# A fixed order for the prologue, the first batch's values summed on GpSimd, queries loaded over ScalarE's queue, and a ring of three token blocks

## The chip, the cores and the metric

One core of a Trainium2 chip runs the whole program. The metric is the device time of one execution in microseconds, as a median of three runs. All arithmetic starts from float32 inputs; the large products are made from pairs of float32r values (a high part and a remainder), three products for each.

## The reference

```
k_p = k.reshape(B, H, Sp, 8, D).mean(axis=3)     # B, H, S, D = 8, 8, 576, 64; Sp = 72
v_p = v.reshape(B, H, Sp, 8, D).mean(axis=3)
attn = softmax(q @ k_p.T / sqrt(D))              # sum + 1e-9 in the denominator
x = (attn @ v_p) as tokens [B * S, H * D]        # 4608 x 512
x = (h - tanh(h)) @ w_out,   h = x @ w_in        # first layer, 512 -> 2048 -> 512
x = (h * cos(h)) @ w_out2,   h = x @ w_in2       # second layer, 512 -> 2048 -> 512
```

## The kernel before

The 4608 tokens are worked through in nine blocks of 512 (`NB`), and in each block over 16 steps `f` of 128 hidden columns (`NF`). A step of either layer makes 12 products into a hidden tile `h` (`emit_h`, line 553; `emit_h2`, line 747), an activation on ScalarE and VectorE (`g1_act`, `g1_rest`, `g_second`; `g2_a`, `g2_b`), and 12 products into four accumulators (`emit_out1`, line 591; `emit_out2`, line 775), two steps later (`LAG`). A finished block of the first layer is copied out of the accumulators (`evac1`, line 598) and stored to `x1s`, and the second layer loads it again (`x1_load`, `x1_split`, spread over the steps by `x1_next`).

Attention makes the first layer's tokens. A tile of up to 128 queries goes through `s1` (transposes of the queries, line 332, and a copy `qT`, line 334), `s2` in two halves (scores, line 346; row maximum, line 349; subtraction, line 353; exponential, line 355), `norm` (sum, add, reciprocal, multiply, lines 360 to 364), `s3` in two parts (transposes of the weights, lines 375 and 385, copies `ah`, `ar`), and, when its group of tiles is complete, `pv` four times (value products, line 406; copy `xh`, line 409; remainder `xl`, line 413). Batches 0 and 1 (`PV32`) make the value products in plain float32. Keys and values come as 8 x 64 rows and are summed by `pool_kv`: for batch 0 by one reduction on VectorE (line 266), for the others by three additions on GpSimd (lines 269, 270). `kprep` transposes the summed keys into `bd`; `place_v` puts the summed values into `vbd` and `vbr`, scaled by the columns of `mk`. Tokens go into `xh` and `xl`, a ring of `RING` columns; `xcols` cuts a stretch of tokens where the ring wraps, and `emit_h` makes a product for each piece.

The weights of the first layer arrive as 64-bit words and are converted on the way (`converter`, run step by step by `w1_tick`): ScalarE line 157, VectorE lines 166 and 168, ScalarE line 172, GpSimd line 149 or 162. Even steps' weights stay on chip (`RES`), odd ones (`STR`) go to DRAM and are streamed through a ring of two tiles each, `ri` and `ro`. The second layer's weights are converted during the first layer's blocks and loaded in the last one by `w2_resident`.

The prologue handles batch 0: its four tiles of 128 queries and the scores of the fifth (64 queries), and the key sums of batch 1. The rest of attention is a list of items; during each block `slot` hands out the items that are due, so that the next block's tokens are ready in time. Up to block 7 a planner with a cost model orders each engine's instructions out of this program (`MANUAL = 8`; from block 8 on the program's own order holds, by `tc.manual_schedule()`), and it may bring work of block 0 forward into the prologue. All loads are issued on SyncE's queue.

## Time and profile before

| what | us |
| --- | --- |
| median of 3 runs | 1791.51 |
| lowest and highest | 1791.44, 1793.8 |
| the profiled execution | 1789.61 |
| its span, first to last instruction | 1787.8 |
| TensorE busy in it | 1741.1 |
| VectorE, ScalarE, GpSimd busy | 1242.3, 1147.4, 276.0 |

The span is what the trace covers; the rest of the profiled execution's time lies around it. Busy time of an engine is the union of its instructions. PE stands for TensorE's matmuls, PEld for its weight loads, DVE for VectorE, ACT for ScalarE, POOL for GpSimd, SP for SyncE; L12 is line 12 of the kernel. Rows of a timeline give the start, the length and, in brackets, the idle time of the engine just before and what ended it.

### The profile page before, as it was taken

How to read it: one execution, taken by the hardware profiler on the slowest of the kernel's cores; microseconds unless marked ns; L12 is line 12 of the kernel's file. 1: busy time of each engine (PE TensorE's matmuls, PEld its weight loads, DVE VectorE, ACT ScalarE, POOL GpSimd, SP SyncE). 2: the span in 40 equal slices, each digit the busy share in tenths (PEclk: the TensorE clock that was granted, in tenths of full speed). 3: DMA queues.
4: the chain of work that ended last, by engine and by line, in shares of the span. 5: the costliest groups of instructions: out<-in, count | busy, mean ns of one | idle time of the engine just before them, and what ended most of it. 6: DMA issues, size and time to landing. Idle time of an engine off the chain costs nothing.

```text
span 1787.8 us, 23298 instructions
## 1 busy us (share of the span) xinstructions
PE 1741.1 (97%) x8344; PEld 1446.7 (81%) x8344; DVE 1242.3 (69%) x2109; ACT 1147.4 (64%) x2079; POOL 276.0 (15%) x342
## 2 busy tenths in 40 slices
PE   4989999999999999999999999999999999999999
PEld 3666878998888888889988888888888888888887
DVE  8689788778888887776666566566656665666555
ACT  4567666767677776765555666666666566666665
POOL 3754244213424131100000000000000000000000
PEclk9799999999999999999999999999999999999999
DMA  7565655545655564523278201010101010101000
GB/s 233 167 211 184 218 165 191 198 158 183 209 180 182 185 199 140 176 99 111 79 258 306 100 12 36 13 42 7 42 7 42 7 41 7 42 7 41 1 24 24
DMA packets 116403, 202.32 MB, mean 113 GB/s; under 512 B 45376, under 2 KB 61760, under 8 KB 116288
## 3 DMA queue, kind: packets, MB, share of 16 engines
q1 hardware_dynamic: 116288, 200.84, 33.9%
q8 instruction: 66, 1.08, 0.3%
q14 instruction: 49, 0.40, 0.1%
HBM read 156.76 MB, written 44.04 MB: 112 GB/s over the span
## 4 chain that ended last, share of the span: by engine, by line
PE 86%; DVE 5%; DMA 3%; ACT 3%; POOL 2%; issue 1%; SPq 0%; POOLq 0%; DVEq 0%; ACTq 0%
PE h L747 22%; PE acc L775 21%; PE h L553 19%; PE acc L591 18%; PE att L406 2%; PE att L346 2%; DMA kv<-in_k_dram 1%; POOL kv L269 1%; DVE cva L168 1%; PE att L375 1%; DMA raw<-in_moe_w_in_dram 1%; DVE w L576 1%; DMA raw<-in_moe_w_out_dram 1%; PE att L332 1%; DVE cva L166 0%
## 5 line engine op out<-in xcount | busy, mean ns | idle before, releaser
L747 PE MATMUL h<-xh,wi 128*128 128x512 f32 x1152 | 378.2, 389 | 0.0
L775 PE MATMUL acc<-wo,gh 128*128 128x512 f32 x1152 | 354.9, 389 | 0.1
L775 PEld LDWEIGHTS acc<-wo,gh 128*128 128x128 f32 x1152 | 216.2, 188 | 45.4 <-ACT gh L583 0.5
L747 PEld LDWEIGHTS h<-xh,wi 128*128 128x128 f32 x1152 | 216.4, 188 | 45.0
L758 DVE SCALAR_TENSOR_TENSOR r<-kk,h 128x512 f32<-128x512 f32 (+1 forms) x145 | 99.2, 684 | 181.9 <-ACT kk L756 181.4
L747 PE MATMUL h<-xl,wi 128*128 128x512 f32 x576 | 224.2, 389 | 0.0
L775 PE MATMUL acc<-wo,gl 128*128 128x512 f32 x576 | 224.2, 389 | 0.0
L766 ACT ACTIVATE r<-r 128x512 f32<-128x512 f32 (+1 forms) x145 | 91.4, 630 | 195.1 <-DVE r L760 195.1
L553 PE MATMUL h<-xh,wi 128*128 128x512 f32 (+1 forms) x704 | 205.9, 364 | 1.8 <-ACT wi L172 1.2
L553 PE MATMUL h<-xh,ri 128*128 128x512 f32 (+1 forms) x704 | 203.3, 360 | 0.0
L572 DVE SCALAR_TENSOR_TENSOR w<-u,h 128x512 f32<-128x512 f32 x144 | 98.3, 682 | 149.3 <-ACT th L565 149.0
L768 DVE TENSOR_TENSOR co<-co,h 128x512 f32<-128x512 f32 (+1 forms) x145 | 99.3, 685 | 117.9 <-ACT co L767 117.9
L591 PE MATMUL acc<-gh,wo 128*128 128x512 f32 x576 | 179.3, 393 | 0.0
L591 PE MATMUL acc<-gh,ro 128*128 128x512 f32 x576 | 177.9, 390 | 0.0
L755 ACT ACTIVATE kk<-h,bias_r 128x512 f32<-128x512 f32 (+1 forms) x145 | 99.5, 686 | 92.0 <-PE h L747 92.0
L564 ACT ACTIVATE u<-h 128x512 f32<-128x512 f32 x144 | 85.7, 595 | 103.9 <-PE h L553 103.5
L553 PEld LDWEIGHTS h<-xh,wi 128*128 128x128 f32 x704 | 126.4, 191 | 19.7 <-ACT wi L172 1.4
L553 PEld LDWEIGHTS h<-xh,ri 128*128 128x128 f32 x704 | 125.4, 190 | 17.2 <-POOL ri L162 0.4
L583 ACT ACTIVATE gh<-w 128x512 fp32r<-128x512 f32 x144 | 90.9, 631 | 74.7 <-DVE w L577 72.6
L584 DVE TENSOR_TENSOR gl<-w,gh 128x512 fp32r<-128x512 f32 x144 | 107.6, 747 | 28.7 <-ACT gh L583 25.9
L775 PEld LDWEIGHTS acc<-wo,gl 128*128 128x128 f32 x576 | 108.0, 188 | 22.5 <-DVE gl L584 0.2
L747 PEld LDWEIGHTS h<-xl,wi 128*128 128x128 f32 x576 | 108.0, 188 | 22.4
(157 smaller groups left out, 3376.0 us busy)
## 6 DMA issues: line engine op xcount, KB each, us to landing
ri<-s1i SPq DMA_DIRECT2D x64, 512.0 KB, 3.5
ro<-s1o SPq DMA_DIRECT2D x64, 512.0 KB, 3.7
raw<-in_moe_w_in_dram SPq DMA_DIRECT2D x32, 512.0 KB, 4.0
raw<-in_moe_w_out_dram SPq DMA_DIRECT2D x32, 512.0 KB, 4.1
x1s<-xe SPq DMA_DIRECT2D x36, 256.0 KB, 4.8
xr<-x1s SPq DMA_DIRECT2D x36, 256.0 KB, 3.0
out_dram<-xe SPq DMA_DIRECT2D x36, 256.0 KB, 2.0
kv<-in_k_dram SPq DMA_DIRECT2D x32, 256.0 KB, 4.0
```

The costliest lines, as they stand in the source:

```text
L553: nc.tensor.matmul(out=h[:, off:off + m], lhsT=wi[:, c, wsel, :], rhs=xt[:, r:r + m], start=(n == 0), stop=(n == 3 * KC - 1))
L564: nc.scalar.activation(out=u, in_=h, func=AF.Square)
L572: nc.vector.scalar_tensor_tensor(w, u, C2, h, op0=ALU.mult, op1=ALU.mult)
L583: nc.scalar.activation(out=gh[:, a:e], in_=w[:, a:e], func=AF.Copy)
L584: nc.vector.tensor_tensor(gl[:, a:e], w[:, a:e], gh[:, a:e].bitcast(F32), op=ALU.subtract)
L591: nc.tensor.matmul(out=acc[d], lhsT=wo[:, wsel, d * 128:(d + 1) * 128], rhs=gt, start=(f == 0 and n == 0), stop=(f == NF - 1 and n == 2))
L747: nc.tensor.matmul(out=h, lhsT=wi[:, c, wsel, :], rhs=xt[:, o:o + BLK], start=(n == 0), stop=(n == 3 * KC - 1))
L755: nc.scalar.activation(out=kk[:, a:e], in_=h[:, a:e], func=AF.Identity, bias=bias_r, scale=INV_2PI)
L758: nc.vector.scalar_tensor_tensor(r[:, a:e], kk[:, a:e], -PI2_HI, h[:, a:e], op0=ALU.mult, op1=ALU.add)
L766: nc.scalar.activation(out=r[:, a:e], in_=r[:, a:e], func=AF.Abs)
L768: nc.vector.tensor_tensor(co[:, a:e], co[:, a:e], h[:, a:e], op=ALU.mult)
L775: nc.tensor.matmul(out=acc[t], lhsT=gt[:, t * 128:(t + 1) * 128], rhs=wo[:, wsel, :], start=(f == 0 and n == 0), stop=(f == NF - 1 and n = ...
```

## The change

The ring holds 1536 columns instead of 1280, so a block always starts at a multiple of 512. To make room the mask of the first layer's activation overwrites its input `u`, the reloads of the first layer's result use the buffers `xe` of the result copies (and come three steps later), and the second layer's weights of the last two odd steps live in the ring tiles. The prologue runs in the program's own order, rewritten by hand; it ends with the four tiles of batch 0 that make the first 512 tokens. The fifth tile's scores and batch 1's key sums become items of block 0. Batch 0's values are summed on GpSimd. The queries of the four tiles are loaded by ScalarE's queue. An exponential on one column stands first on ScalarE, and tiles 2 and 3 have their own buffers for the exponentials, out of the space of `al`, which batches 0 and 1 don't use. Nine conversion steps are asked for in the prologue, where there were 26, of which the rule `w1_allowed` lets through the first six pieces. In the diff the removed lines of the old prologue are left out (they stand in the kernel above).

```diff
--- before.py
+++ after.py
@@ -49,7 +49,7 @@
     NP = H // 2
     BLK = 512
     NB = NT // BLK
-    RING = 1280
+    RING = 1536
     LAG = 2
     RES = [f for f in range(NF) if f % 2 == 0]
     STR = [f for f in range(NF) if f not in RES]
@@ -262,14 +262,15 @@
         else:
             n = GR if b in PV32 else 3 * GR
             o = vr[:n, c - NP, :]
-        if b == 0:
+        if b == 0 and which == "k":
             nc.vector.tensor_reduce(o, t[:n].rearrange("p (r d) -> p d r", r=POOL), axis=AX.X, op=ALU.add)
         else:
             for w in (POOL * D // 2, POOL * D // 4):
                 nc.gpsimd.tensor_tensor(t[:n, :w], t[:n, :w], t[:n, w:2 * w], op=ALU.add)
             nc.gpsimd.tensor_tensor(o, t[:n, :D], t[:n, D:2 * D], op=ALU.add)
-        if which == "k" and c == NKC - 1:
-            nc.scalar.activation(out=kp[:, :, D:2 * D], in_=kp[:, :, 0:D], func=AF.Copy)
+        if which == "k" and (c == NKC - 1 or (b == 0 and c == KSPLIT[0][1] - 1)):
+            c0 = (KSPLIT[1][0] if c == NKC - 1 else 0) if b == 0 else 0
+            nc.scalar.activation(out=kp[:, c0:c + 1, D:2 * D], in_=kp[:, c0:c + 1, 0:D], func=AF.Copy)
 
     def place_v(b):
         if b not in PV32 and b - 1 in PV32:
@@ -317,10 +318,10 @@
                     o = e * SP + x0 - h * SP
                     nc.scalar.activation(out=bd[p:p + D, h // 2, o:o + x1 - x0], in_=at[p:p + D, x0 - lo:x1 - lo], func=AF.Copy)
 
-    def load_q(t, pool=None, tag="qt", bufs=2):
+    def load_q(t, pool=None, tag="qt", bufs=2, queue=None):
         n = t["n"]
         qt = (pool or ap).tile([128, H * D], F32, tag=tag, name="qt", bufs=bufs)
-        nc.sync.dma_start(
+        (queue or nc.sync).dma_start(
             out=qt[:n].rearrange("p (h d) -> p h d", h=H),
             in_=q[t["b"], :, t["s"]:t["s"] + n, :].rearrange("h s d -> s h d"))
         t["qt"] = qt
@@ -334,10 +335,12 @@
         nc.scalar.activation(out=qT[:, :, :n], in_=at.rearrange("p (g n) -> p g n", g=NP)[:, :, :n], func=AF.Copy)
         t["qT"] = qT
 
+    first_e = {}
+
     def s2(t, half):
         n = t["n"]
         if half == 0:
-            t["e"] = eb[t["i"] % 2]
+            t["e"] = first_e.pop(t["i"], eb[t["i"] % 2])
             t["sm"] = ap.tile([128, H], F32, tag="sm", name="sm", bufs=2)
         e, sm, qT = t["e"], t["sm"], t["qT"]
         at = att_tile()
@@ -367,7 +370,8 @@
         n, e, g, o = t["n"], t["e"], t["g"], t["o"]
         if o == 0 and part == 0:
             g["ah"] = ap.tile([128, NP, 320], F32R, tag="ah", name="ah")
-            g["al"] = ap.tile([128, NP, 320], F32R, tag="al", name="al")
+            if t["b"] not in PV32:
+                g["al"] = ap.tile([128, NP, 320], F32R, tag="al", name="al")
             g["ar"] = ap.tile([3 * GR, NG, 320], F32R, tag="ar", name="ar")
         at = att_tile()
         if part == 0:
@@ -375,10 +379,10 @@
                 nc.tensor.transpose(at[:, p * 128:p * 128 + n], e[:n, main_rows(p)], ident[:n, :n])
             av = at.rearrange("p (c n) -> p c n", c=NP)[:, :, :n]
             ah = g["ah"][:, :, o:o + n]
-            al = g["al"][:, :, o:o + n]
             if t["b"] in PV32:
                 nc.scalar.activation(out=ah.bitcast(F32), in_=av, func=AF.Copy)
                 return None
+            al = g["al"][:, :, o:o + n]
             nc.scalar.activation(out=ah, in_=av, func=AF.Copy)
             return lambda: nc.vector.tensor_tensor(al, av, ah.bitcast(F32), op=ALU.subtract)
         for a in range(NG):
@@ -451,7 +455,15 @@
 
 
     t = tiles[n0]
-    item(lambda: kprep(0))
+    item(lambda t=t: s1(t), lambda t=t: load_q(t))
+    post_kv("k", 1, 0)
+    post_kv("k", 1, 1)
+    item(lambda t=t: s2(t, 0), apart=True)
+    post_kv("k", 1, 2)
+    post_kv("k", 1, 3)
+    item(lambda t=t: s2(t, 1))
+    post_kv("k", 1, 4)
+    item(lambda: kprep(0), apart=True)
     post(lambda t=t: norm(t))
     post_kv("v", 1, 0)
     item(lambda t=t: s3(t, 0))
@@ -567,14 +579,13 @@
 
     def g1_rest(h, u, th):
         s = cp.tile([128, BLK], F32, tag="t2", name="s")
-        m = cp.tile([128, BLK], F32, tag="t3", name="m")
         w = cp.tile([128, BLK], F32, tag="t4", name="w", bufs=2)
         nc.vector.scalar_tensor_tensor(w, u, C2, h, op0=ALU.mult, op1=ALU.mult)
         nc.scalar.activation(out=s, in_=u, func=AF.Square, bias=bias_q)
         nc.vector.scalar_tensor_tensor(th, th, -1.0, h, op0=ALU.mult, op1=ALU.add)
-        nc.scalar.activation(out=m, in_=u, func=AF.Relu, bias=bias_m)
+        nc.scalar.activation(out=u, in_=u, func=AF.Relu, bias=bias_m)
         nc.vector.scalar_tensor_tensor(w, s, SQ_D, w, op0=ALU.add, op1=ALU.mult)
-        step_end[0] = nc.vector.copy_predicated(w, m.bitcast(U32), th)
+        step_end[0] = nc.vector.copy_predicated(w, u.bitcast(U32), th)
         return w
 
     def g_second(w, cols):
@@ -712,17 +723,22 @@
     wi2, wo2 = {}, {}
     xraw = {}
 
+    LAST = STR[-2:]
+
     def w2_resident(pool, f):
-        wi2[f] = pool.tile([128, KC, 2, 128], F32R, tag=f"wi{f}", name="wi")
-        wo2[f] = pool.tile([128, 2, DM], F32R, tag=f"wo{f}", name="wo")
+        if f in LAST:
+            wi2[f], wo2[f] = ring_tile_i(), ring_tile_o()
+        else:
+            wi2[f] = pool.tile([128, KC, 2, 128], F32R, tag=f"wi{f}", name="wi")
+            wo2[f] = pool.tile([128, 2, DM], F32R, tag=f"wo{f}", name="wo")
         nc.sync.dma_start(out=rows(wi2[f]), in_=s2i[f])
         nc.sync.dma_start(out=rows(wo2[f]), in_=s2o[f])
 
     def xoff(i):
-        return 0 if i % 2 else RING - BLK
+        return RING - BLK if i % 2 else 0
 
     def x1_load(i, c):
-        xr = cp.tile([128, BLK], F32, tag="xr", name="xr", bufs=2)
+        xr = cp.tile([128, BLK], F32, tag="xe", name="xr", bufs=4)
         nc.sync.dma_start(out=xr, in_=x1s[i][:, c, :])
         xraw[i, c] = xr
 
@@ -733,10 +749,10 @@
         nc.vector.tensor_tensor(xl[c][:, o:o + BLK], xr, xh[c][:, o:o + BLK].bitcast(F32), op=ALU.subtract)
 
     def x1_next(i, f):
-        if f % 3 == 0 and f < 12:
-            x1_load(i, f // 3)
-        if f % 3 == 2 and f < 12:
-            x1_split(i, f // 3)
+        if f % 3 == 0 and f > 0 and f <= 3 * KC:
+            x1_load(i, f // 3 - 1)
+        if f % 3 == 2 and f > 2 and f <= 3 * KC + 2:
+            x1_split(i, f // 3 - 1)
 
     def emit_h2(wi, i):
         o = xoff(i)
@@ -788,83 +804,96 @@
 
     if True:
...
+        with tc.manual_schedule():
+            warm = cp.tile([128, 1], F32, name="warm")
+            nc.vector.memset(bias_q, SQ_B)
+            nc.vector.memset(bias_m, -T * T)
+            nc.vector.memset(bias_r, MAGIC)
+            nc.vector.memset(bias_c, HALF_PI)
+            nc.scalar.activation(out=warm, in_=bias_m, func=AF.Exp)
+            make_identity(nc, ident)
+            for c in range(3):
+                load_k(0, c)
+            load_k(0, 3, cp, "t0", 2)
+            load_k(0, 4, cp, "t0", 2)
+            load_q(tiles[0], queue=nc.scalar)
+            load_q(tiles[1], queue=nc.scalar)
+            w1_load(0)
+            for c, (tag, bufs) in enumerate((("t4", 2), ("t4", 2), ("gh", 3), ("gh", 3), ("gh", 3), ("t2", 1))):
+                load_v(0, c, cp, tag, bufs)
+            load_q(tiles[2], cp, "xe", 4, nc.scalar)
+            load_q(tiles[3], cp, "xe", 4, nc.scalar)
+            for n in range(1, 6):
+                w1_load(n)
+            nc.gpsimd.memset(kp, 0.0)
+            nc.gpsimd.memset(bd, 0.0)
+            values()
+            spare = ap.tile([128, 2, H * SP], F32, tag="al", name="e0")
+            first_e.update({2: spare[:, 0, :], 3: spare[:, 1, :]})
+
+            banks.extend([None, acc[0], "h", acc[1], None, acc[2], "h", acc[3]])
+            for j, (c0, c1) in enumerate(((0, SP), (SP, 128), (0, SP - RR), (SP - RR, 128))):
+                nc.vector.tensor_reduce(mk[:, j:j + 1], ident[:, c0:c1], axis=AX.X, op=ALU.add)
+            nc.vector.tensor_reduce(
+                mk[:, 4:6], ident.rearrange("p (c g i) -> p g c i", g=2, i=RR), axis=AX.XY, op=ALU.add)
+            nc.vector.tensor_scalar(mk, mk, 1.0 / POOL, None, op0=ALU.mult)
+            for c in range(KSPLIT[0][1]):
+                pool_kv("k", 0, c)
+            s1(tiles[0])
+            kprep(0)
+            for c in range(KSPLIT[1][0], NKC):
+                pool_kv("k", 0, c)
+            s1(tiles[1])
+            kprep(1)
+            for c in range(NP + NG):
+                pool_kv("v", 0, c)
+            ex = {}
+
+            def scored(j):
+                ex[j] = (s2(tiles[j], 0), s2(tiles[j], 1))
+
+            def exps(j):
+                for fn in ex.pop(j):
+                    fn()
+
+            scored(0)
+            exps(0)
             w1_tick(2)
+            scored(1)
+            w1_tick(1)
+            exps(1)
+            s1(tiles[2])
+            norm(tiles[0])
+            scored(2)
+            done(s3(tiles[0], 0))
+            done(s3(tiles[0], 1))
+            exps(2)
+            norm(tiles[1])
+            s1(tiles[3])
+            scored(3)
+            done(s3(tiles[1], 0))
+            done(s3(tiles[1], 1))
+            place_v(0)
+            exps(3)
+            norm(tiles[2])
+            w1_tick(1)
+            g = tiles[1]["g"]
+            xs = [pv(g, p) for p in range(NP)]
+            done(s3(tiles[2], 0))
+            done(s3(tiles[2], 1))
+            for fn in xs:
+                fn()
+            norm(tiles[3])
             w1_tick(2)
+            done(s3(tiles[3], 0))
+            done(s3(tiles[3], 1))
+            for p in range(NP):
+                done(pv(tiles[3]["g"], p))
+            w1_tick(3)
         banks.clear()
         w1_until(0)
         early = w1_ticks[0]
@@ -891,7 +920,7 @@
                 if i > 0 or f >= NF - 2:
                     ring_ahead(nsi, ring_load_i, i, f)
                 if i == NB - 1:
-                    if f < len(STR):
+                    if f < len(STR) - len(LAST):
                         w2_resident(bp, STR[f])
                     if f - 3 in RES:
                         w2_resident(cp, f - 3)
@@ -932,8 +961,7 @@
                 else:
                     x1_next(0, f)
         for f in range(NF - 3, NF):
-            if f in RES:
-                w2_resident(cp, f)
+            w2_resident(cp, f)
         for i in range(NB):
             for f in range(NF):
                 h = emit_h2(wi2[f], i)
```

## Rows read from the trace of the kernel before

**Rows 1.** The page: busy time by engine, granted clock in 40 slices, one costly group.

```profile
PE 1741.1 (97%) x8344; PEld 1446.7 (81%) x8344; DVE 1242.3 (69%) x2109; ACT 1147.4 (64%) x2079; POOL 276.0 (15%) x342
...
PEclk9799999999999999999999999999999999999999
...
L572 DVE SCALAR_TENSOR_TENSOR w<-u,h 128x512 f32<-128x512 f32 x144 | 98.3, 682 | 149.3 <-ACT th L565 149.0
```

**Rows 2.** Windows by stage: length, busy us (and instructions) by engine, clock, DMA share, GB/s.

```profile
0.00:59.20 59.20, 33.18 (x124) 22.32 (x125) 44.17 (x85) 26.61 (x62) 29.44 (x42) 0.86 0.62 195
59.20:197.00 137.80, 125.79 (x549) 97.81 (x548) 113.88 (x183) 94.78 (x190) 69.93 (x80) 0.94 0.63 203
197.00:314.50 117.50, 114.34 (x601) 94.36 (x600) 94.33 (x180) 81.49 (x177) 52.65 (x75) 1.00 0.59 188
...
1006.50:1094.00 87.50, 87.50 (x387) 72.46 (x387) 52.83 (x87) 55.45 (x90) 0.00 (x0) 1.00 0.09 28
```

**Rows 3.** Windows, finer, of the first 197 us.

```profile
42.50:59.20 16.70, 11.24 (x25) 5.52 (x26) 9.75 (x17) 6.18 (x14) 14.43 (x20) 0.50 0.31 91
59.20:66.40 7.20, 7.20 (x22) 4.63 (x20) 1.53 (x3) 2.37 (x9) 4.50 (x10) 0.50 0.78 283
...
100.00:150.00 50.00, 43.02 (x186) 32.23 (x186) 47.29 (x71) 35.07 (x67) 29.01 (x30) 0.97 0.65 212
```

**Rows 4.** Timeline of TensorE, first 60 us: start, length, line, operation, idle before.

```profile
9.22 1.09 PE L332 MATMUL att<-ident,qt 128*128 128x128 f32 x4 [9.22 <-DMA qt<-in_q_dram]
...
25.87 1.32 PE L346 MATMUL acc<-bd,qT 128*128 128x144 f32 x4 [5.03 <-ACT qT L334]
...
33.50 0.70 PE L406 MATMUL h<-ah,vbd 128*128 128x256 f32 x2
...
47.70 1.08 PE L375 MATMUL acc<-ident,eb 128*128 128x128 f32 x4 [8.61 <-ACT cva L157]
...
51.77 1.22 PE L406 MATMUL h<-ah,vbd 128*128 128x256 f32 x2
```

**Rows 5.** Groups by form on TensorE: busy us, mean ns, of 256-column matmuls.

```profile
L553 PE MATMUL h<-xh,wi 128*128 128x256 f32 x256 | 49.6, 287 | 0.0
...
L553 PE MATMUL h<-xl,wi 128*128 128x256 f32 x128 | 36.2, 283 | 0.0
```

**Rows 6.** Timeline of TensorE in block 2 and in block 3.

```profile
344.95 0.40 PE L553 MATMUL h<-xh,ri 128*128 128x256 f32 x2
...
347.10 0.28 PE L553 MATMUL h<-xh,ri 128*128 128x256 f32 x1
...
463.34 0.62 PE L553 MATMUL h<-xh,wi 128*128 128x512 f32 x2
...
465.39 0.39 PE L553 MATMUL h<-xh,wi 128*128 128x512 f32 x1
```

**Rows 7.** Timeline of VectorE, first 60 us.

```profile
16.70 1.95 DVE L266 TENSOR_REDUCE va<-kv 128x64 f32<-128x512 f32 x2
...
28.55 0.75 DVE L364 TENSOR_TENSOR eb<-eb,sm 128x576 f32<-128x576 f32 x1
...
32.86 1.48 DVE L364 TENSOR_TENSOR eb<-eb,sm 128x576 f32<-128x576 f32 x1
...
37.51 0.45 DVE L349 TENSOR_REDUCE mx<-att 128x4 f32<-128x288 f32 x1
37.87 0.45 DVE L349 TENSOR_REDUCE mx<-acc 128x4 f32<-128x288 f32 x1
```

**Rows 8.** Timeline of GpSimd, first 60 us.

```profile
32.46 1.26 POOL L162 TENSOR_TENSOR ri<-cva,ri 128x512 fp32r<-128x512 f32 x1 [4.41 <-ACT ri L172]
...
53.19 1.25 POOL L269 TENSOR_TENSOR kv<-kv 128x256 f32<-128x256 f32 x2
...
54.79 1.25 POOL L269 TENSOR_TENSOR kv<-kv 128x256 f32<-128x256 f32 x2
```

**Rows 9.** Timeline of ScalarE, first 60 us.

```profile
9.66 1.28 ACT L272 ACT_TABLE_LOAD   x1 [9.66 <-DVE kp L266]
```

More of the change, by code (lines that the diff above doesn't have):

```diff
@@ L789, in fused_kernel @@
     if True:
-        for c in range(3):
-            load_k(0, c)
-        load_k(0, 3, cp, "t0", 2)
-        load_k(0, 4, cp, "t0", 2)
-        load_q(tiles[0])
-        w1_load(0)
-        w1_load(1)
-        load_q(tiles[1])
-        make_identity(nc, ident)
-        nc.vector.memset(bias_q, SQ_B)
-        nc.vector.memset(bias_m, -T * T)
-        nc.vector.memset(bias_r, MAGIC)
-        nc.vector.memset(bias_c, HALF_PI)
-        nc.gpsimd.memset(kp, 0.0)
-        nc.gpsimd.memset(bd, 0.0)
-        values()
-        for c, (tag, bufs) in enumerate((("t4", 2), ("t4", 2), ("gh", 3), ("gh", 3), ("gh", 3), ("t2", 1))):
-            load_v(0, c, cp, tag, bufs)
-        load_q(tiles[2], cp, "xe", 4)
-        load_q(tiles[3], cp, "xe", 4)
-        load_q(tiles[4], cp, "xe", 4)
-        for n in range(2, 6):
-            w1_load(n)
         def done(fn):
@@ L817, in done @@
                 fn()
-        banks.extend([None, acc[0], "h", acc[1], None, acc[2], "h", acc[3]])
-        for c in range(NKC):
-            pool_kv("k", 0, c)
-        s1(tiles[0])
-        kprep(0)
-        kprep(1)
-        for c in range(NP + NG):
-            pool_kv("v", 0, c)
-        for j, (c0, c1) in enumerate(((0, SP), (SP, 128), (0, SP - RR), (SP - RR, 128))):
-            nc.vector.tensor_reduce(mk[:, j:j + 1], ident[:, c0:c1], axis=AX.X, op=ALU.add)
-        nc.vector.tensor_reduce(
-            mk[:, 4:6], ident.rearrange("p (c g i) -> p g c i", g=2, i=RR), axis=AX.XY, op=ALU.add)
```

35 lines of the change are left out of this document (removed).

## The prediction

> **What bounds the kernel now.** I read the page first. TensorE is busy 97% of the span, so only its idle time and the time it runs at the lower clock can be won, unless it is given less to do; the row of granted clock is below full only in the first slices and the last [rows 1]. Next the windows by stage, cut where the first block's product starts (59.2 us), and where the blocks' results are copied out (197.0, 314.5, a second-layer block at the end). The reader is to see that a second-layer block is gapless, that block 1 has 3.2 us without a matmul, and that the two stretches ahead hold nearly all: 26.0 of the first 59.2 us and 12.0 of the next 137.8 [rows 2]. [...] The timeline of TensorE shows why it matters: a pair of matmuls of the value products lasts 0.70 us at 33.50 and 1.22 at 51.77, and between them lies a pause of 8.61 us, up to 47.70, put down to a ScalarE step of the weight conversion [rows 4]. A value product is two such pairs; I put it at 1.2 us at full clock and 2.3 at half. So the kernel is bound by TensorE from about 200 us on, and before that by a chain through VectorE, ScalarE and GpSimd that starves it. In the stretch from 100 to 150 us VectorE is busy 47.3 of 50 us, TensorE 43.0: there VectorE is the limit [rows 3].
>
> **The ring of 1536 columns.** With 1280, block i starts at 512i modulo 1280, so blocks 2 and 7 wrap and each first-layer product is made in two halves. That shows as 768 matmuls of 256 columns: the two rows given (256 and 128) and two like them for the streamed weights [rows 5]. Price: from 344.95 to 347.10 there are 18 of these, 0.119 us each; whole ones go at (465.39 - 463.34)/9 = 0.228 [rows 6]. Two halves for one whole cost 0.239 - 0.228 = 0.011 us, over 384 pairs 4.3 us. TensorE is gapless there, so 4.3 us come off the end. It costs nothing elsewhere that I find: bytes come from a dropped tile, from reloads sharing the result buffers, and from two second-layer weight pairs living in the ring, which is needed 13 steps after it is free.
>
> **The in-place mask and the later reloads.** The third ScalarE operation of the activation now overwrites its input and has to wait for VectorE's first read of it. The step has a lag of two products; TensorE has no gap in blocks 2 to 8, and work for it stands ready behind. Zero; if the cover were gone, it is one 0.68 us VectorE operation a step [rows 1], over 144 steps 98 us; a second-layer block, whose chain from engine to engine is as long, shows no gap at all [rows 2], so I leave that end out. Reloads of the next block's columns move by three of 16 steps and end one step before the block; a step is 24 x 0.228 = 5.5 us, so nothing waits. Zero from both sides.
>
> **The prologue, head.** Before, the first transposes wait 9.22 us for the first queries [rows 4]. The function table load of 1.28 us at 9.66 goes to the start [rows 9]; but the queries' arrival then ends the wait, and keys and queries now compete from two queues. Bound: 1.3 us sooner, or some 3 us later if they share badly. I grant nothing: first scores at about 13.9 us.
>
> **The prologue, body.** I followed the new order engine by engine, each operation at the duration of its rows. TensorE: scores of tiles 0 and 1 and the third tile's transposes, 5.0 us at the low clock, to 18.9; a 3.0 us wait for the copy of those transposes, which stands on ScalarE behind two exponentials and a conversion step; scores 2, transposes of weights 0, of queries 3, scores 3 with a 0.6 us wait, 7.0 us, to 28.8; transposes of weights 1, 0.7, then 2.6 us until ScalarE has placed the values; four value products, 4 x 1.2 at full clock, to 36.9; weights 2 (0.7), 1.7 us for the last normalization, weights 3 (0.7), 1.7 us for their copies, and four products, to 46.5 us. Against it stands 59.2 before. The order leaves out what the old one did there: scores of tile 4, the second batch's keys, and four of eight converted weight pieces; those go to block 0.
>
> **Values on GpSimd.** VectorE loses six sums of 0.96 us (two take 1.95), 5.7 us in all; GpSimd gains six of 1.6 us (start to start, 53.19 to 54.79), 9.6 us, and at worst twice that where the two contend, as in the rows below [rows 7, 8]. From the values' arrival at about 12 us they end between 22 and 31 and are needed at about 30, by the placing. The work that hides them is scores 1 to 3; if it didn't, the value products would come later by what is over, 1 us at that worst. One more price: VectorE's normalizing multiply takes 0.75 us at 28.55 but 1.48 at 32.86, where GpSimd's subtraction had begun 0.4 us sooner and ended at 33.72 [rows 7, 8]. Three such operations fall into the sums' time, 0 to 2.2 us. [...]
>
> **Queries on ScalarE's queue.** Four issues stand ahead of ScalarE's first copy; the third and fourth could wait for earlier transfers to land. Until the keys are summed ScalarE has nothing to do, so zero; at worst 2 us. With these and the lock I put the first block's first product at 49 us, bounds 46 and 52 at full clock. If the clock stays at half after 28.8, the eight products (1.15 more each) and the transposes add some 10 us: 56 to 61.
>
> **Block 0.** VectorE did 44.2 + 113.9 = 158.1 us up to 197 [rows 2]. Less the 5.7 us, 152.4 are left. In the new prologue it does five key sums (4.8), four tiles at about 3.1 (rows overlap by 0.08: maxima of 0.45 start 0.36 apart; so a maximum and a subtraction as long, twice, 1.5, a multiply of 0.75 and a sum as long 1.4, two small steps 0.2), eight subtractions of 0.35 to 0.4, four conversions at 1.0 and the masks at 1.0, together 25 [rows 7]. So block 0 has 127 us for VectorE where it had 113.9. At the density of 100 to 150 us, 0.946, that is 135 us; at the old block 0's mean, 0.826, 154. TensorE's own need is less: 125.8, of which 3.6 went to the half clock up to 66.4, plus some 2 for tile 4. I take 0.93, near the dense end, since VectorE is now owed work from the first step: 137 us, as long as before (137.8). The block ends at 49 + 137 = 186 instead of 197: 11 us.
>
> **Sum.** 11 + 4.3 = 15.3 us. The profiled execution took 1789.6 us around a span of 1787.8; the median of the three timed runs is 1791.5, 1.9 above, which I keep as offset. The span becomes 1772.5, the time **1776 us**.
>
> **Rivals.** (a) *TensorE sets block 0's pace.* The old contended durations (the 1.48 above) shrink when GpSimd has less to do beside VectorE; then VectorE owes some 8 us less, and full clock from the first step gives 3.6 us more. For it: contention doubled an operation in the rows. Against it: from 100 to 150 us VectorE was the limit at full clock too [rows 3]. Block 0 takes 126, the sum is 22 + 4, the time 1765. (b) *Given back in block 0.* The prologue is shorter only because work left it, and VectorE gets through 127 us at the old mean density: 154 us, end at 203; 6 - 4.3 = +1.7, the time 1793, no change. Against it: that mean includes the stretch from 59 to 66 in which VectorE had 1.5 us of work [rows 3]. (c) *Slower: the clock.* TensorE's pauses of 2 to 3 us keep its clock at half through the prologue, and the first product starts at 58. For it: half clock followed the 8.61 us pause for 19 us of work; against it, the old prologue was at full speed by 33.50, eight microseconds after a pause of 5.03 us [rows 4]. Its price is 9 us; with block 0 at 0.86, 148 us, it ends at 206: +9 - 4.3, the time 1796. It decides once first product and block together pass 205 us. [...] (d) *Only the ring counts*: prologue and block 0 come out even, 1787.
>
> **Chances and range.** Likeliest, 1776 (own range 1768 to 1784): 0.52. (a) 0.22, (b) 0.09, (c) 0.10, (d) 0.07. A measurement of this kernel can tell about 0.2%, 3.6 us, from no change. Cases (a), most of (d) and the likeliest lie below 1787.9: faster 0.79. Within 0.2%: (b) and a little of (d), 0.10; slower 0.11. For 8 in 10 the range takes in (a) with a margin for its lower bound, 1761 (prologue 46, block 0 125, ring), and (d); it ends at 1790, short of (b) and (c).
>
> **What would show it.** Right: no matmul of 256 columns for the first-layer products, 768 fewer of them and 384 more whole; the first block's product starts between 46 and 52; granted clock at full from about 30 us; VectorE over 0.9 busy in the first half of block 0; the first block's copies at about 186; blocks after it as long as before, 2 and 7 about 2 us shorter each. Wrong: a first product at 56 or later at half clock, or block 0 of over 150 us with VectorE idle between its operations, which would make the planner's order, not VectorE's work, its limit; or gaps in the steady blocks, which would mean that the in-place mask or the shared buffers cost what I put at nothing.

## The result, and the profile after

The changed kernel takes 1813.62 us (1811.59 to 1817.39), the kernel before 1791.47 beside it: the ratio is 1.013, interval 1.0113 to 1.0146. It is slower by 22 us where I forecast 15 us faster. The profiled execution took 1817.39 us around a span of 1815.6, 27.8 more than the span of before.

The page after, busy time and granted clock, answering [rows 1]:

```profile
PE 1772.2 (98%) x7960; PEld 1431.9 (79%) x7960; DVE 1233.9 (68%) x2103; ACT 1160.4 (64%) x2081; POOL 286.0 (16%) x360
...
PEclk7699999999999999999999999999999999999999
```

The 384 fewer TensorE instructions are the ring's whole products. Yet TensorE is busy 31 us longer, and after the first two slices the row of granted clock shows 9 (0.9 and more) throughout. Windows by stage, with columns as in [rows 2] and cut at the same events (first product of block 0, copies of blocks 0 and 1, a second-layer block):

```profile
0.00:54.15 54.15, 36.47 (x114) 23.62 (x114) 28.51 (x59) 19.30 (x50) 36.99 (x71) 0.71 0.72 211
54.15:205.00 150.85, 133.75 (x556) 99.37 (x556) 122.88 (x202) 102.98 (x204) 71.08 (x68) 0.92 0.57 185
205.00:324.30 119.30, 115.59 (x574) 94.27 (x573) 92.69 (x179) 82.77 (x178) 51.04 (x74) 0.99 0.58 183
1018.00:1106.50 88.50, 88.50 (x385) 71.90 (x384) 51.94 (x86) 55.16 (x89) 0.00 (x0) 1.00 0.09 30
```

The first product comes 5.1 us sooner than before (54.15 against 59.2), block 0 is 13.1 us longer, and so the first block ends 8 us later. That leaves 20 us behind 205 us, where TensorE has hardly a gap and the clock is 0.99 or 1.00. A step of a second-layer block on TensorE, first in the kernel after, then in the same kernel with the tile `warm` 64 columns wide (experiment `e1_warm64`). The first two rows shown of a fence are the starts of 12 hidden-tile products and of the 12 output products behind them; the third is the seventh output product, the fourth the next step's start:

```profile
1400.90 0.40 PE L763 MATMUL h<-xh,wi 128*128 128x512 f32 x1
...
1403.70 0.63 PE L791 MATMUL acc<-wo,gh 128*128 128x512 f32 x2
...
1405.09 0.62 PE L791 MATMUL acc<-wo,gh 128*128 128x512 f32 x2
...
1406.45 0.40 PE L763 MATMUL h<-xh,wi 128*128 128x512 f32 x1
```

```profile
1400.25 0.39 PE L763 MATMUL h<-xh,wi 128*128 128x512 f32 x1
...
1402.97 0.61 PE L791 MATMUL acc<-wo,gh 128*128 128x512 f32 x2
```

The twelve hidden-tile products take 2.80 us after and 2.72 with the wider tile: 0.233 and 0.227 us each, back to back in both. No wait is shown; each is a little longer. Over the 144 steps of the second layer 0.08 us make 11.5 us. The output products lose less: their first six take 1.39 us, their last six 1.36, which is 0.227 each.

Timeline of TensorE up to block 0's first products and at its longest stall, answering [rows 4]:

```profile
5.53 1.09 PE L333 MATMUL att<-ident,qt 128*128 128x128 f32 x4 [5.53 <-DMA qt<-in_q_dram]
...
11.59 1.33 PE L349 MATMUL att<-bd,qT 128*128 128x144 f32 x4
...
31.00 0.67 PE L410 MATMUL h<-ah,vbd 128*128 128x256 f32 x2 [1.14 <-POOL kv L269]
...
33.48 1.22 PE L410 MATMUL att<-ah,vbd 128*128 128x256 f32 x2
...
44.33 1.22 PE L410 MATMUL h<-ah,vbd 128*128 128x256 f32 x2 [1.13 <-ACT ah L383]
...
54.15 0.79 PE L565 MATMUL h<-xh,wi 128*128 128x512 f32 x1
...
57.30 0.42 PE L565 MATMUL h<-xl,wi 128*128 128x512 f32 x1
...
75.63 2.50 PE L602 MATMUL acc<-gh,ro 128*128 128x512 f32 x5 [3.91 <-ACT gh L594]
```

Windows of the second group of value products and around the stall:

```profile
42.50:54.15 11.65, 10.52 (x25) 4.65 (x23) 2.00 (x5) 3.03 (x8) 8.37 (x15) 0.50 0.34 114
...
67.00:91.50 24.50, 20.59 (x65) 15.04 (x64) 13.98 (x26) 11.82 (x27) 10.30 (x12) 0.65 0.44 138
```

The head is faster than I granted. The first value products go at full clock (a pair in 0.67 to 0.70 us, granted 0.99 from 31.00 to 33.48); from 33.48 a pair takes 1.22 us, at half clock (granted 0.50), and that stays though TensorE has no pause from 44.33 on. First-layer products begin at 54.15, still granted 0.50, and from 57.30 they are at full clock (granted 1.00 up to 62.62). The stall at 75.63 is explained by ScalarE and GpSimd:

```profile
72.41 0.66 ACT L157 ACTIVATE cva<-raw 128x512 f32<-128x512 f32 x1 [4.77 <-POOL wo L162]
72.98 0.70 ACT L586 ACTIVATE u<-u,bias_m 128x512 f32<-128x512 f32 x1
```

```profile
67.06 1.27 POOL L269 TENSOR_TENSOR kv<-kv 128x256 f32<-128x256 f32 x2 [0.51 <-DMA kv<-in_k_dram]
...
69.70 1.45 POOL L269 TENSOR_TENSOR kv<-kv 128x256 f32<-128x256 f32 x2
71.11 1.27 POOL L162 TENSOR_TENSOR wo<-cva,wo 128x512 fp32r<-128x512 f32 x1
```

GpSimd sums keys from 67.06 to 71.1; the conversion's remainder (L162) stands behind them; ScalarE's next conversion step waits for it up to 72.41, and the activation's mask (L586, 72.98) stands behind that. Block 0 here waits for a chain from engine to engine, in which GpSimd's sums stand ahead of the remainder; ScalarE is idle for 4.77 us of it and TensorE for 3.91.

### The profile page after: what moved, and what is told of

The parts are those of the page before. It is cut to its first block, busy times and chain, and to the rows that moved or that the text cites. A ratio compares the mean times of both kernels' runs of the same rounds, so it can differ in the third digit from the quotient of the medians.

```text
span 1815.6 us, 22634 instructions
## 1 busy us (share of the span) xinstructions
PE 1772.2 (98%) x7960; PEld 1431.9 (79%) x7960; DVE 1233.9 (68%) x2103; ACT 1160.4 (64%) x2081; POOL 286.0 (16%) x360
## 3 DMA queue, kind: packets, MB, share of 16 engines
q10 hardware_dynamic: 4160, 1.05, 0.3%
## 4 chain that ended last, share of the span: by engine, by line
PE 88%; DVE 4%; DMA 3%; POOL 2%; ACT 2%; issue 2%; SPq 0%; POOLq 0%; DVEq 0%; ACTq 0%
PE h L763 22%; PE acc L791 22%; PE h L565 19%; PE acc L602 18%; PE att L410 2%; PE att L349 2%; DMA kv<-in_k_dram 2%; DVE cva L168 1%; POOL kv L269 1%; PE att L379 1%; PE att L333 1%; DVE w L588 1%; DVE w L587 1%; DVE cva L166 0%; DVE w L583 0%
## 5 line engine op out<-in xcount | busy, mean ns | idle before, releaser
L763 PE MATMUL h<-xh,wi 128*128 128x512 f32 x1008 | 337.5, 396 | 0.0
L791 PE MATMUL acc<-wo,gh 128*128 128x512 f32 x1008 | 312.9, 392 | 0.0
L763 PEld LDWEIGHTS h<-xh,wi 128*128 128x128 f32 x1008 | 189.1, 188 | 45.4
L791 PEld LDWEIGHTS acc<-wo,gh 128*128 128x128 f32 x1008 | 189.5, 188 | 42.7
L565 PE MATMUL h<-xh,wi 128*128 128x512 f32 x576 | 200.5, 409 | 6.5 <-POOL wi L162 4.3
L565 PE MATMUL h<-xh,ri 128*128 128x512 f32 x576 | 201.3, 409 | 4.1 <-POOL ri L162 2.9
L763 PE MATMUL h<-xl,wi 128*128 128x512 f32 x504 | 199.5, 396 | 0.0
L583 DVE SCALAR_TENSOR_TENSOR w<-u,h 128x512 f32<-128x512 f32 x144 | 98.3, 683 | 147.7 <-ACT th L577 147.5
L791 PE MATMUL acc<-wo,gl 128*128 128x512 f32 x504 | 196.1, 389 | 0.0
L565 PEld LDWEIGHTS h<-xh,wi 128*128 128x128 f32 x576 | 108.8, 190 | 32.1 <-POOL wi L162 6.3
L602 PEld LDWEIGHTS acc<-gh,ro 128*128 128x128 f32 x576 | 109.1, 190 | 28.7 <-ACT gh L594 4.7
L588 DVE COPY_PREDICATED w<-u,th 128x512 f32<-128x512 uint32 x144 | 114.8, 797 | 23.5 <-ACT u L586 11.1
L602 PEld LDWEIGHTS acc<-gh,wo 128*128 128x128 f32 x576 | 109.0, 190 | 24.5 <-ACT gh L594 0.2
```

The source lines that it names most:

```text
L565: nc.tensor.matmul(out=h[:, off:off + m], lhsT=wi[:, c, wsel, :], rhs=xt[:, r:r + m], start=(n == 0), stop=(n == 3 * KC - 1))
L583: nc.vector.scalar_tensor_tensor(w, u, C2, h, op0=ALU.mult, op1=ALU.mult)
L588: step_end[0] = nc.vector.copy_predicated(w, u.bitcast(U32), th)
L602: nc.tensor.matmul(out=acc[d], lhsT=wo[:, wsel, d * 128:(d + 1) * 128], rhs=gt, start=(f == 0 and n == 0), stop=(f == NF - 1 and n == 2))
L763: nc.tensor.matmul(out=h, lhsT=wi[:, c, wsel, :], rhs=xt[:, o:o + BLK], start=(n == 0), stop=(n == 3 * KC - 1))
L791: nc.tensor.matmul(out=acc[t], lhsT=gt[:, t * 128:(t + 1) * 128], rhs=wo[:, wsel, :], start=(f == 0 and n == 0), stop=(f == NF - 1 and n = ...
```

## Experiments

Each time is a median, unless said otherwise, beside the kernel before on the same chip (1790.25 to 1791.01 us there); ratios have their 95% interval. "Block 0" is the length from the first first-layer product to the first copy of its result.

### What makes every product longer

The one new tile ahead of the weights is `warm`, a single column. The built program gives it 32 bytes behind the ring, and `u`, `gh`, `gl` and the weight tiles, all at multiples of 256 bytes before, lie 32 past them; the ring does not move. Six kernels set this apart.

```diff
# e1_warm64, from the kernel after
-            warm = cp.tile([128, 1], F32, name="warm")
+            warm = cp.tile([128, 64], F32, name="warm")
# e2_pad32, from the kernel before; e6_pad64 and e7_pad128: PAD = 16, 32
+    PAD = 8
+    xl = [cp.tile([128, RING + (PAD if c == KC - 1 else 0)], F32R, name=f"xl{c}") for c in range(KC)]
# e3_shift32, from the kernel before: the ring moves too
+    bias_c = cp.tile([128, 16], F32, name="bias_c")[:, 0:1]
# e11_weights32, from the kernel before: th and r, behind gh and ahead of gl
+        th = cp.tile([128, BLK + 8], F32, tag="t1", name="th")[:, :BLK]
```

> The changed kernel, with the one-column tile for the first exponential made 64 columns wide, so that every tile allotted behind it lies 224 bytes further on, again at a multiple of 256 bytes from the start of a partition, as all of them do in the kernel before; the work is the same. Theory A (the place of the weights, 32 bytes off, slows the matmuls): a second-layer block takes 87.0 us again instead of 88.7, the products of the hidden tile start 0.227 us apart instead of 0.235, and the time is 1787 to 1791 (1813.6 less 24). Rival B (the longer ring itself, another place of the moving columns or the two weight pairs in the ring tiles slows them): blocks stay at 88.7 us, the time at 1813.

> The kernel before, with 32 unused bytes behind the last tile of the ring, so that the moving columns of the hidden products keep their place and all weights and activation tiles lie 32 bytes further on. Theory A: a second-layer block takes 88.7 us instead of 87.0, the time becomes 1816 to 1821 (18 blocks at 1.5 more, 27). Rival B: 1791, nothing changes.

> The kernel before, with 32 more bytes ahead of the ring, so that the moving columns and the weights all lie 32 bytes further on and keep their distance. If it is the distance between moving columns and weights that counts (A1): 1791, a block 87.0 us. If each tile's own place counts (A2): 1816 or more, with the products out of the hidden tile slow as well. Rival B: 1791.

> The kernel before with 64 unused bytes behind the ring instead of 32. If the distance between moving columns and weights has to be a multiple of 64 bytes, products start 0.227 us apart and the time is 1791; if it has to be a multiple of 128 or 256, a block takes 88.7 us or something between, and the time is 1800 to 1820.

> The kernel before with 128 unused bytes behind the ring. If the distance between moving columns and weights has to be a multiple of 128 bytes: products 0.227 us apart, 1791. If of 256: as with 32 and 64 bytes, a block near 88.7 us, about 1810.

> The kernel before with the tile of the tanh 32 bytes longer: what lies ahead of it (the ring, u, w, gh, the results, the weights of steps 0 and 2) keeps its place, what lies behind (the low parts gl, the weights of all other steps, the streamed ones) moves by 32 bytes. Theory A1 (weights against the moving columns): in the second layer the hidden products of steps 0 and 2 start 0.227 us apart, those of the other resident steps 4 to 14 0.235. If instead it is the activation tiles, ahead of all, that disturb TensorE: all steps 0.227, 1791.

Measured: `e1_warm64` 1791.58 us, 1.0004 (0.9991 to 1.0018). A tile of 256 bytes instead of 32 gives back 22 us, with the same work. (Executions of these two kernels differ in the mean clock that they are granted, and the time follows it: at 0.988 to 0.990 the changed kernel took 1811.59 and 1812.04, `e1_warm64` 1785.54 to 1787.46, so at a like clock it is 25 us.) `e2_pad32` 1809.48, 1.0107 (1.009 to 1.0124): the kernel before, with 32 bytes nobody reads, has the loss too. `e3_shift32` 1790.63, 1.0004 (0.9994 to 1.0013): with the ring shifted as well, nothing is lost. So in these runs it is not a tile's own place that counts, but how far apart the tiles lie. One execution each: `e6_pad64` 1810.45, `e7_pad128` 1805.93: 64 and 128 bytes are bad too. Copies out of the accumulators on ScalarE, `e2_pad32`, then `e4_steady` (below), whose tiles are aligned; the first first-layer block, then two second-layer blocks:

```profile
196.55 2.06 ACT L599 ACTIVATE xe<-acc 128x512 f32<-128x512 f32 x4
...
1099.30 1.07 ACT L784 ACTIVATE xe<-acc 128x512 f32<-128x512 f32 x2
1188.05 1.07 ACT L784 ACTIVATE xe<-acc 128x512 f32<-128x512 f32 x2
```

```profile
196.25 0.60 ACT L597 ACTIVATE xe<-acc 128x512 f32<-128x512 f32 x1
...
1087.56 1.07 ACT L787 ACTIVATE xe<-acc 128x512 f32<-128x512 f32 x2
1174.60 1.07 ACT L787 ACTIVATE xe<-acc 128x512 f32<-128x512 f32 x2
```

A second-layer block takes 88.75 us and 87.04. The first 196 us differ by 0.3: there, where TensorE waits for others, the longer products don't show.

`e11_weights32` took 1820.61 in one execution. It leaves the tokens and `gh` in place and moves `gl` and the weights by 32 bytes, save the weights of steps 0 and 2, which lie ahead of the wider tile. TensorE in steps 0 and 1 of a second-layer block, first and last of the twelve hidden-tile products, and then the twelve output products up to step 2:

```profile
1183.64 0.39 PE L747 MATMUL h<-xh,wi 128*128 128x512 f32 x1
...
1186.15 0.39 PE L747 MATMUL h<-xh,wi 128*128 128x512 f32 x1
1189.17 0.40 PE L747 MATMUL h<-xh,wi 128*128 128x512 f32 x1
...
1191.73 0.40 PE L747 MATMUL h<-xh,wi 128*128 128x512 f32 x1
1191.97 0.63 PE L775 MATMUL acc<-wo,gh 128*128 128x512 f32 x2
...
1194.76 0.39 PE L747 MATMUL h<-xh,wi 128*128 128x512 f32 x1
```

Eleven spacings take 2.51 us with the unmoved weights of step 0 and 2.50 with those of step 2, and 2.56 with the moved ones of step 1, in one block of one kernel; three steps with moved weights, from 1295.22 on, have 2.57, 2.56 and 2.56. The output products bear it out: the twelve take 2.79 us here, where `gh` stays and the weights move, and 2.75 in the kernel after, where both lie 32 bytes on; this fits the longer time of this run beside `e2_pad32`. So in these runs the distance between the columns that stream and the weights sets the pace, 0.228 us a product or 0.233. Why, no run shows.

### The ring without the prologue

`e4_steady` is the kernel before with the ring, the in-place mask, the shared reload buffers and the last weights in the ring; prologue and items as before.

> The kernel before, with the change's second half alone: ring of 1536, mask in place, reloads in the result buffers, last weight pairs in the ring tiles; the old prologue, no tile for a first exponential, so that all tiles keep multiples of 256. Theory A and the prediction's term: 4.3 us faster than before, 1787, blocks of the second layer 87.0 us. Rival B: about 1791.5 + 27 - 4 = 1814, blocks 88.7 us.

Measured 1785.83 us, 0.9976 (0.9965 to 0.9986): 4.6 us faster. The first product starts at 59.2, block 0 takes 137.1. This version beats both kernels.

### The parts of the prologue, in the new order and in the old

```diff
# e9_vdve, from e1_warm64; e17_old_vgp: the reverse, from e4_steady
-        if b == 0 and which == "k":
+        if b == 0:
# e10_qsync, from e1_warm64; e18_old_q: the reverse, from e4_steady
-            load_q(tiles[0], queue=nc.scalar)
+            load_q(tiles[0])
...
# e19_old_both: e17_old_vgp and e18_old_q together
```

> The changed kernel with the 64-column tile of e1, and the first batch's values summed by one reduction on VectorE again. [...] If, as predicted, it is hidden: VectorE is idle for more than 10 us ahead of 31 us, GpSimd comes free earlier, and the time stays within 2 us of 1791.6.

> The changed kernel with the 64-column tile of e1, and all queries loaded on SyncE's queue again, in the same place of the program. If the second queue gives the head of the prologue what the trace shows (first transposes at 5.8 us instead of 9.2): first scores 1 to 2 us later than 11.5, and the time 1 to 3 us longer than 1791.6. If the keys' sums end the wait anyway (prediction): within 1 us.

> The kernel with the ring and its companions and the old prologue (e4, 1785.83 us), with one part more: the first batch's values summed on GpSimd. Theory M: each move helps by itself, whatever the order; in the fixed order this one was worth 6 us (1797.8 to 1791.6), so 1780 to 1783. Theory N: the gain belongs to the fixed order, where VectorE is what the first products wait for; in the old order the long pause of TensorE ahead of the third tile's transposes ends with a ScalarE step, so within 2 us of e4; or it loses some 3 to 10 us, because GpSimd is then held by sums when batch 1's keys and the weights' pieces come.

> e4 with one part more: the queries of the first four tiles loaded by ScalarE's queue, order as before. Theory M: the first transposes start at about 5.8 us instead of 9.2, and 3 us or more of it reach the end: about 1780 to 1783. Theory N: the first scores wait for the summed keys, which are no sooner; first scores within 1 us of before, time within 2 us of e4; or the keys are late because both queues share the DMA engines, and it loses 1 to 3 us.

> e4 with both parts. Theory M: the two gains add up, 1775 to 1780. Theory N: within 3 us of e4 or slower.

Measured: `e9_vdve` 1797.82 us, 1.0044 (1.003 to 1.0057), 6 us slower than `e1_warm64`, and `e10_qsync` 1798.02, 1.0035 (1.0022 to 1.0048). In the new order each part is worth some 6 us, but not in the same place. In `e9_vdve` the first product comes at 60.9 us instead of 52.7 and block 0 is as long (146.6); in `e10_qsync` it comes at 53.4, and block 0 takes 152.3 us; its profiled execution was granted 0.983 on the mean, that of `e1_warm64` 0.989. (One execution of `e10_qsync`, granted 0.987 where the others were granted 0.983 or 0.984, took 1791.36, so part of its 6 us goes with the clock.) With the sums on VectorE, TensorE waits long for the third tile's queries; their copy stands on ScalarE behind the first exponentials, and these wait for VectorE (6.36 us, up to 18.62):

```profile
25.24 1.33 PE L349 MATMUL acc<-bd,qT 128*128 128x144 f32 x4 [9.47 <-ACT qT L335]
```

In the old order the same parts cost 5 us of what `e4_steady` gained: `e17_old_vgp` 1790.86, 1.0005 (0.9995 to 1.0014), `e18_old_q` 1791.84, 1.0008 (0.9997 to 1.0019), both 1792.25, 1.0011 (1.0002 to 1.0021). TensorE in `e17_old_vgp` ahead of the third tile's weights:

```profile
53.51 1.09 PE L375 MATMUL acc<-ident,eb 128*128 128x128 f32 x4 [11.51 <-ACT cva L157]
```

This pause was 8.61 us before [rows 4]; first products come at 65.0 instead of 59.2. In `e18_old_q` they come at 63.0: the pause is shorter, 4.76, but the first group of value products, from 32.73, takes 1.19 to 1.22 us a pair (0.70 in [rows 4] at 33.50), and from 53.27 on a pair takes 1.22 again. The two gains belong to the fixed order. (Why the planner's order reacts so to each was not followed further.)

### Clock and conversions

Aligned, the new prologue stands at 1791.58 us against 1785.83 with the old one (the executions of the first spread from 1785.54 to 1797.4; the two profiled spans, 1785.5 and 1783.7, are nearer to each other). The spread goes with the clock: three executions granted 0.989 or 0.990 on the mean took up to 1787.46, the seven granted 0.982 to 0.985 took 1791.13 and more, while all eight of `e4_steady` were granted 0.988 to 0.991. So most of the 5.75 us goes along with the lower clock of most executions of the new prologue; no run shows which of the two brings the other. What follows compares two profiled executions of nearly the same clock, 0.989 and 0.991. What TensorE waits for in block 0, in `e1_warm64` and in `e4_steady` (us in total, times, longest):

```profile
PE h L565 <- POOL wi L162: 4.0, 4, 2.0
PE acc L602 <- ACT gh L594: 4.0, 1, 4.0
PE h L565 <- POOL ri L162: 3.0, 5, 1.0
PE h L565 <- ACT wi L172: 2.3, 2, 1.7
```

```profile
PE att L375 <- DVE eb L353: 5.7, 2, 3.8
PE att L406 <- DVE xl L413: 3.7, 1, 3.7
PE att L346 <- DVE eb L353: 1.7, 1, 1.7
...
PE h L553 <- POOL wi L162: 0.6, 1, 0.6
```

With the new prologue hidden-tile products wait 9.3 us in these rows for converted weights (L162, L172); with the old one 0.6. Windows from first product to first copy, `e1_warm64` and `e4_steady`:

```profile
52.70:199.60 146.90, 128.92 (x556) 96.02 (x556) 123.40 (x202) 102.73 (x203) 71.30 (x68) 0.96 0.60 190
```

```profile
59.20:196.30 137.10, 123.52 (x547) 95.29 (x546) 114.99 (x182) 94.92 (x189) 73.41 (x80) 0.95 0.63 203
```

VectorE is given 8.4 us more and its busy share is the same, 0.84; at that share 8.4 us are 10, about what block 0 has grown by. Six kernels ask whether the clock or the late conversions are the cause:

```diff
# e8_ticks, from e1_warm64: a conversion step after each of the last four value products
+                l4 = pv(tiles[3]["g"], p)
+                w1_tick(1)
+                done(l4)
# e12_fill, from e1_warm64: 16 products that nobody reads, 3 + 1 + 1 + 1 in each group of value products, 4 between
+            xs = [filled(1 if p else 3, g, p) for p in range(NP)]
...
# e13_fill_ticks: both
# e14_cut_new, from e1_warm64, and e15_cut_old, from e4_steady
-                        out=h[:, off:off + m], lhsT=wi[:, c, wsel, :], rhs=xt[:, r:r + m],
+                        out=h[:, off:off + m], lhsT=wi[:, c, 0, :], rhs=xt[:, r:r + m],
...
# e16_early, from e1_warm64: three steps in each of six places, one after each of the last value products
+            w1_tick(3)
...
+        return f in RES or step1[0] >= f - 2 or f == 3
```

> The changed kernel with the 64-column tile of e1, and four more conversion steps in the prologue, one behind each of the last four value products, so that the weights of steps 0 to 2 are converted before block 0 as in the old prologue. Theory C (block 0 stalls because the converted weights come late, and the clock falls behind the stall): the pauses of 1.7, 0.8 and 4.0 us between 62 and 76 us go, the half clock at 75 too; the first block is copied out at 190 to 194 instead of 199.6, the time is 1783 to 1787 instead of 1791.6. Theory D (what is short is VectorE's time or GpSimd's in block 0 as a whole, wherever the conversions stand): the pauses come later instead, 1790 to 1793.

> The changed kernel with the 64-column tile of e1, and 17 products more in the prologue whose results nobody reads (the converted weights of step 0 against themselves, float32r, 512 columns): 3 ahead of each group of value products, 1 between two of them, 4 ahead of the last transposes of weights, where TensorE mostly waits. Theory E (the value products run at half clock because TensorE was too little used; cost some 8 us): half clock ends before 40 us, the first block's product starts at 46 to 49 instead of 52.7, the time is 1784 to 1788 instead of 1791.6. Rival F (the clock stays low whatever stands between them, or block 0 takes the gain back): each extra product costs 0.2 to 0.4 us, first product at 55, 1791 to 1797.

> The same with the four conversion steps of e8 behind the last value products. Theory E with C: both gains, 1781 to 1785, below the kernel with the old prologue and the new ring (1785.8). If block 0 is bound by its own chain of conversions, and what is gained ahead of it is lost in it: as e12 or above, 1787 or more.

> The changed kernel with the 64-column tile of e1, in which the first layer's products take the high part of the weights in place of the low part, and the high part is the first ScalarE operation's result without VectorE's bits (but for steps 1 and 2), so that TensorE waits for two ScalarE operations instead of the whole conversion; all the conversion's operations stay, on the same engines. Theory G: block 0 takes 120 to 130 us instead of 147, the time is 1764 to 1775, and it is 4 to 9 us faster than e15, since the 6.5 us of the prologue now reach the end. Theory H: block 0 stays above 140, the time is above 1783, and e15 stays some 6 us faster.

> The same edit of the weights in e4, the old prologue with the new ring. Theory G: block 0 takes 125 to 132 us instead of 137, the time is 1772 to 1781. Theory H: 1780 to 1786, faster than e14.

> The changed kernel with the 64-column tile of e1, and the conversion steps of eight pieces (steps 0 to 3) spread over the prologue, where VectorE and ScalarE are idle half of the time; step 3's pieces are let through. Theory G: the conversions have the lead of the old prologue again, block 0 takes 136 to 140 us behind a first product at 53 to 55, the time is 1780 to 1785, at or below e4's 1785.8. Theory H: VectorE's work in block 0 falls by 5 us, the time is about 1787. If the conversions hold up the prologue's own chain: first product at 57 or later, 1788 or more.

Measured, in the order above:

| kernel | us | ratio, interval | first product | block 0 |
| --- | --- | --- | --- | --- |
| `e8_ticks` | 1789.22 | 0.9995, 0.9987 to 1.0004 | 53.6 | 147.7 |
| `e12_fill` | 1790.63 | 0.9994, 0.9983 to 1.0006 | 54.2 | 147.3 |
| `e13_fill_ticks` | 1791.25 | 1.0011, 1.0001 to 1.002 | 54.5 | 148.3 |
| `e14_cut_new` | 1786.77 | 0.9984, 0.997 to 0.9999 | 49.0 | 142.7 |
| `e15_cut_old` | 1789.16 | 0.9993, 0.9984 to 1.0002 | 58.1 | 135.3 |
| `e16_early` | 1803.45 | 1.0077, 1.0064 to 1.0091 | 66.1 | 147.3 |

(In `e12_fill` and `e13_fill_ticks` the low parts of the first 256 tokens are read from accumulators that were written again; the amount of work is kept.)

Four steps more (`e8_ticks`) only move the stall from about 75 us to 71.7, where it ends with a converted weight. The extra products (`e12_fill`) keep the first group of value products at 0.59 to 0.69 us a pair, but take the time that this gives; after the next pause, 3.55 us, the second group has pairs of 1.05 to 1.22:

```profile
34.36 0.69 PE L410 MATMUL acc<-ar,vbr 32*128 32x256 f32 x2
...
40.34 1.12 PE L379 MATMUL acc<-ident,e 128*128 128x128 f32 x4 [3.55 <-DVE e L367]
...
43.08 1.22 PE L410 MATMUL att<-ah,vbd 128*128 128x256 f32 x2
```

`e14_cut_new` and `e15_cut_old` leave the remainder out of the first layer: they use the high weights twice and, but for steps 1 and 2, take them from ScalarE's first operation, so that no product waits for the whole conversion. This takes 4.2 us off block 0 with the new prologue and 1.8 off with the old (behind block 0, ordered anew, they are 5.3 and 6.2 us longer, so that `e15_cut_old` isn't faster). Block 0 is still 7.4 us longer with the new prologue than with the old, instead of 9.8. So waiting for the remainder is a part of the loss, and the smaller one. Converting more in the prologue (`e16_early`) holds up its own chain, since the steps stand among the copies and maxima of the same engines (TensorE waits 5.82 us for one):

```profile
53.52 1.08 PE L379 MATMUL att<-ident,e 128*128 128x128 f32 x4 [5.82 <-ACT cva L157]
```

The waits for weights in its block 0 then come to 1.9 us in the rows of 0.8 or more, and VectorE has 117.4 us of work there instead of 123.4; the block is still 147.3, granted 0.89 on the mean (0.75 from 66.1 to 100) where that of `e1_warm64` was granted 0.96. So VectorE's work alone doesn't set its length either. What holds block 0 near 147 us when one wait is taken away is not settled: another appears, and no run with the new prologue gave VectorE over 0.87 there.

## Why the prediction was wrong

**"It costs nothing elsewhere that I find" and "blocks after it as long as before".** This step failed and decides the sign. I counted bytes, not places. The one-column tile, on which the first exponential works and which got no price, puts the weights 32 bytes off the tokens; the twelve hidden-tile products of each of the 288 steps are up to 3% longer (2.80 us against 2.72), the twelve output products some 1% (2.75 against 2.72), and 22 us are lost (1813.62 against 1791.58). The windows of before show block times at an alignment that I never asked about. No rival had it. Without it the forecast would have failed too, by the body and by block 0 below: 1791.58 is no gain.

**Ring: −4.3.** Right; `e4_steady` gives −4.6, and with it mask, reloads and weights in the ring at zero.

**Prologue, head: zero.** First transposes at 5.53 us instead of 9.22, first scores at 11.59 instead of my 13.9 (the kernel before had them at 13.26). Of that ScalarE's queue gave only a part: without it, in `e10_qsync`, they come at 12.61, against 11.80 in `e1_warm64`. The 6 us that it is worth at the end lie behind the first product, where I looked for none.

**Prologue, body: 49.** First products came at 54.15, aligned at 52.7. The order of waits was as I followed it and the first value products started at 31.00, near my estimate of 32. The term mis-sized is the eight value products, 1.2 us each at full clock: the four from 31.00 took 7.1 us and the four from 44.33 took 9.2, instead of 4.8 and 4.8; the first two, granted 0.99, took 2.48. Their price at half clock, 1.15 us more each, was in my bounds and in rival (c), not in the sum. The low clock that the sum names for the first scores is not shown: after, their four groups took 1.17 to 1.33 us each, at a granted 1.00 from 11.59 to 15.59.

**Values on GpSimd, hidden.** Right, and `e9_vdve` shows 6 us. The bound of 2.2 us for contention was not used: the normalizing multiply at 20.23, amid the sums, took 0.83 us, and 0.76 at 25.49, with GpSimd idle. GpSimd paid instead: its sum at 20.53, begun during the multiply, took 0.71 us, and the like one at 22.52 took 0.31. So 0.40 us fell on the sum, which began later, and 0.07 on the multiply. The lock that my 49 us for the first product counts with is shown by no run; what the runs show of the two engines side by side is lengths: these, and the multiply's 1.48 us in [rows 7].

```profile
20.23 0.83 DVE L367 TENSOR_TENSOR eb<-eb,sm 128x576 f32<-128x576 f32 x1
...
25.49 0.76 DVE L367 TENSOR_TENSOR eb<-eb,sm 128x576 f32<-128x576 f32 x1
```

```profile
20.53 0.71 POOL L270 TENSOR_TENSOR vr<-kv 32x64 f32<-32x64 f32 x1
...
22.52 0.31 POOL L270 TENSOR_TENSOR vr<-kv 32x64 f32<-32x64 f32 x1
```

**Block 0: 137 us at a density of 0.93.** VectorE's work was right: in `e1_warm64` 28.3 and 123.4 us, 151.7 in all, against my 152.4. The density failed: 0.84, as in the old block 0, and with 123.4 us that is 146.9. I argued that owed work fills VectorE; but much of the work moved into block 0 is a chain through three engines, on which its first steps wait. The sign that I had named for this, a block 0 of over 150 us with VectorE idle in it, came in the changed kernel (150.85). That was rival (b), and `e1_warm64` at 1791.58 is near its 1793. Against `e4_steady` the new prologue gains 6.5 us up to the first product and loses 9.8 in block 0; what else holds block 0 at 143 to 148 us in the runs that take one wait away is open.

## What to carry over

When a change moves tiles in SBUF, compare the places of streamed and stationary operands as well as the bytes: one column of padding cost 22 us here, more than everything else in this change, and a look at the spacing of products in a steady block shows it (0.233 us against 0.227). Work taken out of a bound stretch isn't won until it has a place; price it at the density that the next stretch has shown (0.84 here), not at the best minutes of it (0.93). A part that helps in one order of instructions can cost as much in another (two parts here are worth some 6 us each in the new order and cost 5 and 6 in the old), so it is tried in the order in which it will run.

## What the runs showed of the hardware

In these runs a 512-column product follows the last at 0.227 us where weights and streamed columns lie a multiple of 256 bytes apart (`e1_warm64`), and at 0.233 where they lie 32 bytes off one (the kernel after); no wait is shown for it. At 64 and 128 bytes the kernel before takes 1810.45 and 1805.93 us (`e6_pad64`, `e7_pad128`, one execution each). In the kernel after, value products back to back from 44.33 us ran at half clock (granted 0.50) to their end at 53.5 us; it was full again (1.00) 3.15 us after the first-layer products began (57.30 against 54.15).
